# Block 0's rows: another order and eight DMA engines for the load, V written back in token order

## The chip, the cores and the metric

The kernel runs on one core of one Trainium2 chip. The metric is the device time of one execution in microseconds (us). Three runs of the kernel before gave 236.09, 236.26 and 236.44 us (median 236.26). The profiled execution took 236.12 us, of which 234.88 us lie between its first and its last instruction (its span); times inside the profile count from the span's start.

## The reference

One input x of 2048 tokens x 512 features (bf16) goes through a layer normalisation, and two branches are added to x:

```python
def _A_ref(x, wqkv, wo):        # 32 heads of 16, window of 8 tokens, every second token
    qkv = (x @ wqkv).reshape(B, S, 3, H, Dh) ...
    idx = pos[:, None] - (jnp.arange(8) * 2)[None, :]          # masked where < 0
    logits = einsum('bhsd,bhswd->bhsw', q, k[idx]) * scale     # softmax over w
    o = einsum('bhsw,bhswd->bhsd', attn, v[idx])
    return o.reshape(B, S, D) @ wo

def _B_ref(x, w_in, w_sp, b_sp, w_out):
    z = gelu(x @ w_in); z1, z2 = z[..., :896], layernorm(z[..., 896:])
    g = einsum('ts,bsf->btf', w_sp, z2) + b_sp[None, :, None]
    return (z1 * g) @ w_out

xn = layernorm(x)
return x + _A_ref(xn, A_wqkv, A_wo) + _B_ref(xn, B_w_in, B_w_sp, B_b_sp, B_w_out)
```

## The kernel before, in words

The 2048 tokens are 16 blocks of 128 rows; a block's rows lie on the 128 partitions. The kernel is written as a list of tasks, each with an engine, what it reads and writes, and an estimated time. A planner in the kernel's own code (`Plan.schedule`) puts the tasks of each engine into an order, by estimated times, priorities, a few landing times written in by hand and lists of names that must follow one another; `Plan.emit` then writes one instruction stream per engine with semaphore waits. SP, ACT and POOL issue the DMAs: plain loads and stores and DMA transposes on SP, block 0 and block 1 of x on ACT, V's write-back on POOL.

The start is what the change touches. TensorE first runs seven matmuls without use (`warm0` to `warm6`, L582), which keep it busy until x arrives. `ldx0` (L563, ACT's queue) loads block 0 of x, `ldx1` (L536, ACT's queue) block 1, `ldwv0` and `ldwv1` (L540, SP's queue) the two halves of V's weights, `ldx2`, `ldx3` and so on the rest (L536, SP's queue), `ldwin2a` and `ldwin2b` the weights of z2.

Blocks 0 to 2 take a short cut for V. TensorE transposes the raw rows by a matmul with an identity (`pe_tr`, L601; tasks `xTx0a`, `xTx0b`, `xTx0c` for block 0, `xTx1`, `xTx2`): the rows of x are the stationary operand, the identity is what is streamed. ACT copies the result out (L628, L632; the tile `xcT`), and V is computed from the raw transposed rows (L704; `V0_0`, `V0_0b`, `V0_1`). ACT evicts it with each row's factor 1/sigma (L712; `vraw`). Much later, when the sum over V's weight columns is known, VectorE takes away the mean's part for blocks 0 to 2 (`fix0` to `fix2`, L759), and the three blocks are written to `vscr` in DRAM (`Vw0` to `Vw2`, L691), one row of 512 elements per token. V of the other blocks goes there directly. Attention later reads `vscr` eight times shifted (`ldVs0` and on, L1005).

Meanwhile VectorE computes the mean and variance of each block's rows (`bnst0`, L621; `bnag0`, L623; `vpe0`, L636), POOL 1/sigma (L638), VectorE the normalised rows (`norm0`, L650; tile `xn`). Block 0's normalised rows are transposed on TensorE as well (`xTr0`, L601 again, between V1 and V2), and ACT copies them into `xnT` (L609); the other blocks go through DMA transposes (L644). From `xnT` come z2 (L836), Q and K (L728) and z1 (L882); then the spatial matmul (L982) and the output (L1038, L1047).

The order on TensorE at the start is written out by hand: warm0 to warm6, xTx0a, xTx0b, xTx0c, warm7, V0_0, V0_0b, xTx1, V0_1, xTx2, V1_0, V1_1, xTr0, V2_0, V2_1, z2_0 and so on.

Of the kernel before, what the change touches and what calls it, by code (L numbers as in the profile page):

```python
# [346 lines left out]
def build_kernel(nc, A_x, A_wqkv, A_wo, B_x, B_w_in, B_w_sp, B_b_sp, B_w_out, out, report=False, emit=True):  # L347
# [14 lines left out]
    x2 = A_x[0]  # L362
    o2 = out[0]

    vscr = nc.dram_tensor("vscr", (16 + S, 512), BF).ap()
# [45 lines left out]
    with ExitStack() as es:  # L411
# [5 lines left out]
        def A(name, n, o2_=0):  # L417
            return ar[:, off[name] + o2_: off[name] + o2_ + n]

        def AC(o_, dims):  # L420
            return bass.AP(tensor=ar, offset=o_, ap=[[AR, 128]] + [list(d) for d in dims])

        def Fv(name, n, o2_=0):
            return fp[:, foff[name] + o2_: foff[name] + o2_ + n]
# [7 lines left out]
        def P(bk, n, o_=0):  # L432
            return ps[:, bk.col(o_): bk.col(o_) + n]
# [65 lines left out]
        def c_mm(n):  # L499
            return max(26.0, n / 2.4 + 2.7)  # L500

        def c_act(n, psum=True, accum=False):
            return (170.0 if psum else 205.0) + n * 0.833 + (200.0 if accum else 0.0)
# [9 lines left out]
        def dma(eng, fn, nbytes, chan, reads=(), writes=(), name="", xbar=False, prio=0.0, after=()):  # L513
            return T(eng, fn, reads=reads, writes=writes, name=name, prio=prio, after=after,
                     dma=dict(chan=chan, nbytes=nbytes, xbar=xbar, iss=(1270.0 if nbytes < 400000 else 2200.0) if xbar else None))

        ident = A("ident", 128)
# [39 lines left out]
        def ld_wqk(which, eng):  # L557
# [2 lines left out]
                A_wqkv[:, 512 * which: 512 * which + 512].rearrange("(c p) n -> p c n", p=128)),  # L560
                512 * 512 * 2, ("wqk", which), writes=[("wqk", which)], name="ld%s" % ("qk"[which]))

        dma("act", lambda e: e.dma_start(A("xin", 512), x2[0:128, :]), 128 * 512 * 2, ("xin", 0),  # L563
            writes=[("xin0", 0), ("xin0", 1)], name="ldx0")
        ld_x(1, "act")
        ld_wv(0)
# [25 lines left out]
        cen = []  # L592
        vps = []

        def pe_tr(src, keys, name, dcs=(0, 1, 2, 3)):
            bk = plan.bank(name)

            def tr(t):
                last = None
                for dc in dcs:  # L600
                    last = t.matmul(P(bk, 128, 128 * dc), src[:, 128 * dc:128 * dc + 128], ident, start=True,  # L601
                                    stop=True)
                return last
            T("pe", tr, reads=keys + ["ident"], writes=[bk], est=len(dcs) * c_mm(128), name=name)
            return bk

        def to_xnT(b, bk, halves, prio=0, after=()):
            for d0, dn in (((0, 2), (2, 2)) if halves else ((0, 4),)):
                T("act", (lambda d0, dn: lambda a: a.activation(  # L609
                    AC(off["xnT"] + d0 * S + 128 * b, [[S, dn], [1, 128]]),  # L610
                    P(bk, 128 * dn, 128 * d0).rearrange("p (c n) -> p c n", c=dn), ACTF.Copy))(d0, dn),
                  reads=[bk], writes=([("xnT", b, d0 // 2)] if halves else [("xnT", b)]), est=c_act(128 * dn),
                  name="xTe%d_%d" % (b, d0), prio=prio)

        def ln_block(b):
            sl = b % 8
            xin = A("xin", 512, 512 * b)
            xn = A("xn", 512, 512 * sl)
            xk = [("xin", b)] if b else [("xin0", 0), ("xin0", 1)]

            T("dve", lambda v: v.bn_stats(Fv("st6", 6, 6 * b), xin), reads=xk, writes=[("st6", b)],  # L621
              est=685, name="bnst%d" % b, prio=b * 0.1)
            T("dve", lambda v: v.bn_aggr(Fv("mv", 2, 2 * b), Fv("st6", 6, 6 * b)), reads=[("st6", b)],  # L623
              writes=[("mv", b)], est=178, name="bnag%d" % b, prio=-1 + b * 0.1)
            if b < NRAW:
                bcs = [pe_tr(xin, xk, "xTx0a", (0,)), pe_tr(xin, xk, "xTx0b", (1,)), pe_tr(xin, xk, "xTx0c", (2, 3))] if b == 0 else [pe_tr(xin, xk, "xTx%d" % b)] * 2
                for c0 in (0, 1) if b == 0 else ():
                    T("act", (lambda c0, bc: lambda a: a.activation(A("xcT", 128, 128 * c0), P(bc, 128, 128 * c0), ACTF.Copy))(c0, bcs[c0]),  # L628
                      reads=[bcs[c0]], writes=[("xcTq", c0)], est=c_act(128), name="xTc0_0%s" % "ab"[c0], prio=-1)
                for h0, hn in ((1, 1),) if b == 0 else ((0, 1), (1, 1)) if b < 2 else ((0, 2),):  # L630
                    bc = bcs[-1 if b == 0 else h0]
                    T("act", (lambda h0, hn, bc: lambda a: a.activation(A("xcT", 256 * hn, 512 * b + 256 * h0),  # L632
                                                                        P(bc, 256 * hn, 256 * h0), ACTF.Copy))(h0, hn, bc),
                      reads=[bc], writes=[("xcT", b, hf) for hf in range(h0, h0 + hn)], est=c_act(256 * hn),
                      name="xTc%d_%d" % (b, h0), prio=-1)
            T("dve", lambda v: v.tensor_scalar(Fv("vpe", 1, b), Fv("mv", 1, 2 * b + 1), LN_EPS, None, ALU.add),  # L636
              reads=[("mv", b)], writes=[("vpe", b)], est=140, name="vpe%d" % b, prio=-1.5 + b * 0.1)
            lnr.append(T("pool", lambda g: g.tensor_tensor(Fv("rstd", 1, b), Fv("vpe", 1, b), Fv("mhalf", 1), ALU.pow),  # L638
                         reads=[("vpe", b), "mhalf"], writes=[("rstd", b)], est=550, name="rstd%d" % b, prio=0))
            norm(b)  # L640
            if b < NXT:
                to_xnT(b, pe_tr(xn, [("xn", sl)], "xTr%d" % b), b == 0)
                return None
            return dma("sp", lambda e: e.dma_start_transpose(AC(off["xnT"] + 128 * b, [[S, 4], [1, 128]]), xn),  # L644
                       128 * 512 * 2, ("xT", sl), reads=[("xn", sl)], writes=[("xnT", b)], name="xTd%d" % b,
                       xbar=True, prio=1)

        def norm(b, after=None):
            xin = A("xin", 512, 512 * b)
            norms.append(T("dve", lambda v: v.tensor_scalar(A("xn", 512, 512 * (b % 8)), xin, Fv("mv", 1, 2 * b),  # L650
                                                            Fv("rstd", 1, b), ALU.subtract, ALU.mult),
                           reads=([("xin", b)] if b else [("xin0", 0), ("xin0", 1)]) + [("mv", b), ("rstd", b)],
                           writes=[("xn", b % 8)], est=c_ts(512), name="norm%d" % b, prio=-1 + b * 0.1,
                           after=([after] if after is not None else ())))
# [33 lines left out]
        fixes = []  # L688

        def v_write(b, vn, vk):  # L690
            dma("pool", lambda e: e.dma_start(vscr[16 + 128 * b: 16 + 128 * b + 128, :], vn),  # L691
                128 * 512 * 2, ("vwr", b % 8), reads=[vk], writes=[("vscr", b)], name="Vw%d" % b, prio=1)

        def v_block(b):
# [61 lines left out]
        def fix_all():  # L756
            for b, vn, vk in fixes:
                def fix(b=b, vn=vn, vk=vk):
                    T("dve", lambda v: v.scalar_tensor_tensor(vn, ncs, Fv("mr", 1, b), vraw(b), ALU.mult, ALU.add),  # L759
                      reads=["ncs", "mr", ("vraw", b)], writes=[vk], est=690, name="fix%d" % b, prio=1)  # L760
                fix()
                v_write(b, vn, vk)
# [131 lines left out]
        for b in range(8, NB):  # L894
            lastx = ld_x(b)
        lnd = [ln_block(b) for b in range(NRAW)]
        mean_rstd()
        csbank = plan.bank("cs", 2)
        for b in range(NRAW):
            v_block(b)  # L900
        lnd += [ln_block(b) for b in range(NRAW, NB)]

        dma("pool", lambda e: e.dma_start(vscr[0:16, :], ar[0:16, off["zeros"]: off["zeros"] + 512]), 16 * 512 * 2,
# [39 lines left out]
        for j in range(NJ):  # L943
            for pr in PAIRS:
# [3 lines left out]
                                                             ap=[[0, 128], [1, S]])),  # L948
# [166 lines left out]
def bass_parallel_sum__sliding_local_dilated__mixer_gmlp__prompt_kernel(  # L1115
    nc, A_x, A_wqkv, A_wo, B_x, B_w_in, B_w_sp, B_b_sp, B_w_out, out
):
    build_kernel(nc, A_x, A_wqkv, A_wo, B_x, B_w_in, B_w_sp, B_b_sp, B_w_out, out)
# [28 lines left out]
```

## Time and profile before

| what | value |
|---|---|
| median of three runs | 236.26 us (236.09 to 236.44) |
| profiled execution | 236.12 us, span 234.88 us |
| TensorE (PE) busy | 230.9 us, 98% of the span |
| VectorE (DVE) busy | 207.2 us, 88% |
| ScalarE (ACT) busy | 96.0 us, 41% |
| L563, issue of block 0's load, on ACT | 0.80 us, 0.43 us long |
| from that issue to landing | 2.7 us |
| block 0's statistics (L621) start | 3.54 us |
| first transpose of block 0 (L601) starts | 3.65 us |
| first V matmul of block 0 (L704) starts | 4.37 us |
| L691, V's write-back: issue, landing | 0.54 us each, 4.0 us (median of 16) |

How to read it: PE is TensorE's matmuls, PEld its weight loads, which run beside them; a letter q behind an engine (ACTq, SPq) marks its instruction queue, where DMAs are issued. In the chain of work that ended last, each line is a start, a length and a group of instructions that followed one another; "issue" is time in which the engine waited for nothing that the profile shows. The ends of matmuls are modelled, their starts are recorded. A row of a transfer is one packet in the trace's packet records, and each DMA engine that took part reports its end by one update of the transfer's semaphore; the consumer waits for the last.

### The profile page before, as it was taken

The numbers are of one execution on the slowest core, as the hardware profiler recorded it, in microseconds if no ns is written. First come the engines' busy times: TensorE is split into PE (matmuls) and PEld (weight loads), VectorE is DVE, ScalarE is ACT, GpSimd is POOL, SyncE is SP. The second block draws the span as 40 slices with busy tenths as digits, with TensorE's granted clock in tenths as the row PEclk, the third lists the DMA queues.
The fourth block names the chain that finished last, engine by engine and source line by source line (L and its number), as shares of the span: only waits on it lengthen the run. The fifth ranks groups of instructions, "written<-read, shape, count | busy, mean of one in ns | idle before, by whom it ended". The sixth has DMA issues, their size and how long they took to land.

```text
span 234.9 us, 2982 instructions
## 1 busy us (share of the span) xinstructions
PE 230.9 (98%) x1107; PEld 109.0 (46%) x1127; DVE 207.2 (88%) x271; ACT 96.0 (41%) x144; POOL 29.3 (12%) x58
## 2 busy tenths in 40 slices
PE   8999999999999999999999999999999999999996
PEld 3545455544444444444444444444444444444443
DVE  4706899999999999999999999998899998999723
ACT  3798878888986589510020532011111111000000
POOL 2305640404261202000000000000000000000000
DMA  6769934999811275345299999999969959945442
GB/s 205 219 197 372 175 68 99 217 190 226 230 47 47 67 238 170 63 123 147 74 358 219 282 208 260 190 230 274 300 187 273 305 138 307 290 116 156 112 137 68
DMA packets 83991, 44.55 MB, mean 190 GB/s; under 512 B 56180, under 2 KB 83204, under 8 KB 83976
## 3 DMA queue, kind: packets, MB, share of 16 engines
q1 hardware_dynamic: 82744, 41.94, 70.6%
q0 software_dynamic: 800, 2.11, 2.9%
q10 hardware_dynamic: 432, 0.30, 0.4%
q8 instruction: 9, 0.15, 0.3%
q14 instruction: 6, 0.05, 0.1%
HBM read 26.62 MB, written 4.22 MB: 131 GB/s over the span
## 4 chain that ended last, share of the span: by engine, by line
PE 98%; issue 1%; DVE 0%; DVEq 0%
PE ps L982 41%; PE ps L728 12%; PE ps L836 10%; PE ps L882 10%; PE ps L1047 10%; PE ps L704 6%; PE ps L1038 6%; PE ps L582 1%; PE ps L772 1%; PE ps L601 1%; DVE arena L1053 0%; PE ps L783 0%; DVEq L325 0%
## 5 line engine op out<-in xcount | busy, mean ns | idle before, releaser
L982 PE MATMUL ps<-arena 128*128 128x512 bf16 x439 | 96.6, 379 | 0.5
L982 PEld LDWEIGHTS ps<-arena 128*128 128x128 bf16 x448 | 43.7, 98 | 53.1 <-issue 0.4
L990 ACT ACTIVATE arena<-ps 128x1024 bf16<-128x1024 f32 (+1 forms) x16 | 14.7, 917 | 76.9 <-PE ps L982 70.5
L749 DVE TENSOR_TENSOR arena<-arena 128x4096 bf16<-128x4096 bf16 x16 | 36.5, 2285 | 0.0
L1010 DVE TENSOR_TENSOR arena<-arena 128x4096 bf16<-128x4096 bf16 x16 | 36.5, 2286 | 0.0
L1013 DVE TENSOR_TENSOR arena<-arena 128x2048 bf16<-128x2048 bf16 (+1 forms) x32 | 30.1, 953 | 0.2
L728 PE MATMUL ps<-arena 128*128 128x512 bf16 x124 | 28.2, 379 | 0.3 <-issue 0.2
L754 DVE TENSOR_TENSOR arena<-arena 128x4096 bf16<-128x4096 bf16 x12 | 27.5, 2290 | 0.1
L1047 PE MATMUL ps<-arena 128*128 128x512 bf16 (+2 forms) x116 | 26.5, 366 | 0.1
L836 PE MATMUL ps<-arena 128*128 128x448 bf16 x128 | 25.5, 352 | 0.0
L882 PE MATMUL ps<-arena 128*128 128x512 bf16 x110 | 24.4, 379 | 0.1
L728 PEld LDWEIGHTS ps<-arena 128*128 128x128 bf16 x128 | 14.4, 113 | 13.3 <-ACT arena L718 0.4
L737 ACT ACTIVATE arena<-ps 128x1024 bf16<-128x1024 f32 x16 | 16.2, 1021 | 6.9 <-PE ps L728 6.8
L1053 DVE TENSOR_TENSOR arena<-ps,arena 128x512 bf16<-128x512 f32 (+2 forms) x17 | 11.2, 659 | 8.6 <-PE ps L1047 8.5
L836 PEld LDWEIGHTS ps<-arena 128*128 128x128 bf16 x128 | 12.5, 98 | 12.1
L1047 PEld LDWEIGHTS ps<-arena 128*128 128x128 bf16 x119 | 11.4, 98 | 12.8
L882 PEld LDWEIGHTS ps<-arena 128*128 128x128 bf16 x112 | 11.0, 98 | 13.2
L1038 PE MATMUL ps<-arena 128*128 128x512 bf16 (+2 forms) x68 | 16.6, 366 | 0.1
L704 PE MATMUL ps<-arena 128*128 128x512 bf16 x62 | 16.2, 391 | 0.1
L844 ACT ACTIVATE arena<-ps 128x896 bf16<-128x896 f32 x16 | 14.6, 913 | 3.4 <-PE ps L836 3.3
L621 DVE BATCH_NORM_STATS2 fpool<-arena 128x6 f32<-128x512 bf16 x16 | 10.7, 685 | 5.8 <-DMA arena<-in_A_x_dram 5.8
L888 ACT ACTIVATE arena<-ps 128x1024 bf16<-128x1024 f32 (+1 forms) x16 | 14.0, 919 | 4.4 <-PE ps L882 4.3
(65 smaller groups left out, 168.5 us busy)
## 6 DMA issues: line engine op xcount, KB each, us to landing
arena<-vscr SPq DMA_DIRECT2D x16, 1024.0 KB, 6.2
arena<-in_A_x_dram SPq DMA_DIRECT2D x30, 128.0 KB, 3.9
vscr<-arena POOLq DMA_DIRECT2D x16, 128.0 KB, 4.0
out_dram<-arena SPq DMA_DIRECT2D x15, 128.0 KB, 2.0
arena<-in_A_wqkv_dram SPq DMA_DIRECT2D x2, 512.0 KB, 4.5
arena<-in_B_w_in_dram SPq DMA_DIRECT2D x2, 448.0 KB, 5.1
arena<-in_B_w_in_dram SPq DMA_DIRECT2D x1, 896.0 KB, 8.3
arena<-in_B_w_out_dram SPq DMA_DIRECT2D x1, 896.0 KB, 5.6
```

Source lines behind the costliest of these rows:

```text
L704: last = t.matmul(P(bk, 512), A("xcT", 128, 512 * b + 128 * dc) if b < NRAW else xTv(b, dc), A("wv", 512, 512 * dc), start=(dc == 0), stop ...
L728: last = t.matmul(P(bk, 512, 512 * which), AC(off["wqk"] + 2048 * which + 512 * dc + c, [[4, 128]]), AC(off["xnT"] + dc * S + 512 * j, [[1 ...
L737: T("act", lambda a: a.activation(AC(qo, [[ko - qo, 2], [1, 512]]), P(bk, 1024).rearrange("p (t n) -> p t n", t=2), ACTF.Copy, scale=0.5), ...
L749: T("dve", (lambda pbv, qb, kb: lambda v: v.tensor_tensor(pbv, qb, kb, ALU.mult))(pbv, qb, kb), reads=rd, writes=[("pb", s_)], est=c_tt(40 ...
L754: T("dve", (lambda av, bv: lambda v: v.tensor_tensor(av, av, bv, ALU.add))(av, bv), reads=[("pb", 1)], writes=[("pb", acc)], est=c_tt(4096 ...
L836: last = t.matmul(P(bk, 448, 512 * hf), xTv(b, dc), AC(off["w_in2"] + 896 * dc + 448 * hf, [[1, 448]]), start=(dc == 0), stop=(dc == 3))
L882: last = t.matmul(P(bk, 512, 512 * i), AC(off["w_in1"] + 896 * dc + 128 * fc, [[1, 128]]), AC(off["xnT"] + dc * S + 512 * j, [[1, 512]]), ...
L982: last = t.matmul(P(bk, 512, 512 * i), AC(off["z2"] + FH * sh + 128 * fc, [[1, 128]]), AC(off["wT%d" % r_] + sh * 512, [[1, 512]]), start= ...
L1010: T("dve", lambda v: v.tensor_tensor(tv, tv, av, ALU.mult), reads=[("attn", b)], writes=[("Vs", sv)], est=c_tt(4096), name="pv%d" % b, pri ...
L1013: T("dve", (lambda n: lambda v: v.tensor_tensor(A("Vs", n, 4096 * sv), A("Vs", n, 4096 * sv), A("Vs", n, 4096 * sv + n), ALU.add))(n), wri ...
L1038: last = t.matmul(P(bk, cn), AC(off["OT"] + 512 * tb + 128 * cc, [[1, 128]]), AC(off["wo"] + 512 * cc + c0, [[1, cn]]), start=(cc == 0), s ...
L1047: last = t.matmul(P(bk, cn), AC(off["z1T"] + fc * S + 128 * tb, [[1, 128]]), AC(off["w_out"] + 512 * fc + c0, [[1, cn]]), start=False, sto ...
```

## The change

Three places change, all for block 0. The load `ldx0` reads the rows in another order: `rows0` turns the 128 rows into 8 groups of 16, the row 8q + a going to partition 16a + q. The leading dimension of the DMA's source is then 8 instead of 128, so the transfer is dealt to eight DMA engines instead of 16. Everything that works row by row (the statistics, the normalisation, the raw V of block 0, its correction) now works on the rows in the new order. Two steps bring the tokens back into order: `xTr0` streams the identity with its columns rearranged (column 8q + a of the result is row 16a + q), and `Vw0` writes the rows of V through the same `rows0` pattern.

```diff
-        dma("act", lambda e: e.dma_start(A("xin", 512), x2[0:128, :]), 128 * 512 * 2, ("xin", 0),
+
+        def rows0(ap):
+            return ap.rearrange("(q a) n -> a q n", a=8)
+
+        dma("act", lambda e: e.dma_start(A("xin", 512), rows0(x2[0:128, :])), 128 * 512 * 2, ("xin", 0),
             writes=[("xin0", 0), ("xin0", 1)], name="ldx0")
...
-        def pe_tr(src, keys, name, dcs=(0, 1, 2, 3)):
+        def pe_tr(src, keys, name, dcs=(0, 1, 2, 3), rhs=None):
             bk = plan.bank(name)
+            rhs = ident if rhs is None else rhs
...
-                    last = t.matmul(P(bk, 128, 128 * dc), src[:, 128 * dc:128 * dc + 128], ident, start=True,
+                    last = t.matmul(P(bk, 128, 128 * dc), src[:, 128 * dc:128 * dc + 128], rhs, start=True,
                                     stop=True)
...
-                to_xnT(b, pe_tr(xn, [("xn", sl)], "xTr%d" % b), b == 0)
+                to_xnT(b, pe_tr(xn, [("xn", sl)], "xTr%d" % b,
+                                  rhs=ident.rearrange("p (a q) -> p q a", a=8) if b == 0 else None), b == 0)
...
         def v_write(b, vn, vk):
-            dma("pool", lambda e: e.dma_start(vscr[16 + 128 * b: 16 + 128 * b + 128, :], vn),
+            rows = vscr[16 + 128 * b: 16 + 128 * b + 128, :]
+            dma("pool", lambda e: e.dma_start(rows0(rows) if b == 0 else rows, vn),
                 128 * 512 * 2, ("vwr", b % 8), reads=[vk], writes=[("vscr", b)], name="Vw%d" % b, prio=1)
```

The tasks, their engines, their estimates and the planner's inputs are the same, so every engine has the same instructions in the same order.

## The prediction

> **What bounds the kernel now.** I read the page first: span, shares, chain.
>
> ```profile
> span 234.9 us, 2982 instructions
> PE 230.9 (98%) x1107; PEld 109.0 (46%) x1127; DVE 207.2 (88%) x271; ACT 96.0 (41%) x144; POOL 29.3 (12%) x58
> ...
> PE 98%; issue 1%; DVE 0%; DVEq 0%
> ```
>
> TensorE is busy for 98% of the span and is 98% of the chain that ended last. So the change counts only through what it does to TensorE: how early its real work starts, how long its own instructions take, and whether it later waits. Next the chain in order of time over the first 9 us, where block 0 is worked on.
>
> ```profile
> 0.84 2.82 PE ps L582 x7
> 3.66 0.57 PE ps L601 x4
> 4.24 0.11 PE ps L582
> 4.34 0.03 issue
> 4.37 1.01 PE ps L704 x2
> 5.38 0.43 PE ps L601 x4
> 5.81 0.64 PE ps L704 x2
> 6.45 0.22 PE ps L601 x4
> 6.67 0.86 PE ps L704 x4
> 7.54 0.22 PE ps L601 x4
> ```
>
> L582 is warm-up work without use, L601 a transpose of four 128-column matmuls, L704 V. Two things are to be seen. First, the same four L601 matmuls take 0.43 us at 5.38 and 0.22 us at 6.45: TensorE runs at half speed until about 6.1 us. By the start times in the trace (5.605, 6.031, 6.288) the L704 matmul at 6.031 has a pitch of 0.257 us between the slow 0.427 and the fast 0.216; with t us of it slow, t + (0.427 - t) x 0.216/0.427 = 0.257 gives t = 0.08. Second, from 4.37 on the pieces join without a gap, and the start times go on so to 232.75: besides records that are missing, no matmul starts more than about 0.12 us late. A shift at the start therefore reaches the end.
>
> The third view is the timeline around block 0's arrival.
>
> ```profile
> 3.54 0.69 DVE L621 BATCH_NORM_STATS2 fpool<-arena 128x6 f32<-128x512 bf16 x1 [2.35 <-DMA arena<-in_A_x_dram]
> 3.62 0.35 PEld L601 LDWEIGHTS ps<-arena 128*128 128x128 bf16 x4 [0.55 <-issue]
> ...
> 3.95 0.45 ACT L628 ACTIVATE arena<-ps 128x128 bf16<-128x128 f32 x2 [0.71 <-PE ps L601]
> ...
> 4.34 0.21 PEld L704 LDWEIGHTS ps<-arena 128*128 128x128 bf16 x2 [0.27 <-issue]
> ```
>
> VectorE and TensorE both start block 0 right after its load (L563, issued at 0.80). Its sixteen semaphore updates in the trace come in two groups: eight at 2.78 to 2.86, eight at 3.36 to 3.52. The last one lets bnst0 go at 3.54 and the first weight load at 3.62. The warm-up would let TensorE go at 3.46 (its last matmul starts at 3.351, pitch 0.107). So the load holds TensorE for 0.19 us, no more; ACT's copy (3.95 to 4.23) then sets V0's start at 4.37.
>
> **The change part by part.**
>
> *The load.* Still 128 rows of 1 KB, but with a leading dimension of 8, so 16 rows on each of 8 engines instead of 8 on 16. An undisturbed row takes 46 ns in the packet records. The early group got its 8 rows done in 0.58 to 0.65 us (first packet 1.865, semaphore packets 2.443 to 2.523), because from 2.1 us wv's rows from SP's queue take turns with it. By 2.1 us five rows per engine are through; the other 11, taking turns, need 11 x 2 x 0.046 = 1.01, so 3.1 to 3.27 with the spread seen; 0.34 us from semaphore packet to landing gives 3.45 to 3.61, against 3.516. That holds if the eight are the early ones; I take it so, because a transfer that is dealt out from its first row on reaches the early group first, and eight engines counted from there are that group. The bounds: 0.74 us for 16 undisturbed rows lands at 2.95 (the gain stops at 0.19 us); a load that lies on few engines already, wo's (L964: four engines by its semaphore updates, 32 rows each), landed 3.0 to 3.7 us after issue, which here is 4.5. I take the middle of the first estimate, no shift.
>
> [...]
>
> *What a shift costs.* Start later by d while the clock rises at the same moment, and work worth d at half speed remains to be done at full speed: d/2. If the clock's rise moves along, it is d.
>
> *What follows on the queues.* Early engines get 8 rows more, 0.37 us, late ones as much less. Their landings say what that meets: wv's second half landed at 4.44 to 4.92 and 4.98 to 5.30, and would land at 4.8 to 5.3 and 4.6 to 4.9; V0_1 needs it at 5.6. x1 (4.38, needed at 5.18 by TensorE, 4.55 by VectorE) and x2 (5.64, needed at 6.29) keep theirs within 0.1. Cost nothing, while that cover of 0.2 us or more holds. wo's loads, on fewer engines too, were issued in 0.53 to 0.62 us against 0.43: 0.1 to 0.2 us more on ACT's queue in front of x1's issue, the table load and the first activation; these end at 3.24, ACT is first needed at 3.95, cover 0.7.
>
> *The identity read.* xTr0 (7.54 above) must undo the order: its four matmuls now stream the identity with a step of 16 elements, 32 bytes. TensorE has no gap there, so every ns counts, four times. No matmul of the trace streams with such a step; the nearest is the weight load that reads with a step of 4 elements:
>
> ```profile
> L728 PEld LDWEIGHTS ps<-arena x128: 112/113/132, 17.6 to 78.5; 128*128 128x128 bf16 x128
> L836 PEld LDWEIGHTS ps<-arena x128: 97/98/98, 8.2 to 64.2; 128*128 128x128 bf16 x128
> ```
>
> 15% more: 4 x 55 x 0.15 = 0.03 us. At half rate, the pace of the slow clock above, it is 0.43 - 0.22 = 0.21 us. I take 0.2, since the step is four times as wide; zero and 0.66 (quarter rate: 4 x 3 x 0.055) are the ends.
>
> [...]
>
> *V's write-back.* Vw0 goes out on POOL at 89.17 with the same 128 rows, in token order; it landed at 91.18, and its reader ldVs0 is issued on SP at 103.02. Even at three times its 2 us, cover remains: nothing. Statistics, raw V and the correction of block 0 are per row and move with the rows.
>
> *Sum, of the profiled run* (236.12 us, span 234.88): + 0 (load) + 0.2 (identity) = 236.3. The median of the three is 236.26, so 236.45. 0.2% is 0.47 us, about what a measurement can tell.
>
> **Rivals.**
>
> *Early data, early clock.* Block 0 lands by 3.35 and fills the 0.19 us hole. For it: half of its rows are there at 2.86. On its own that is worth 0.1 to 0.19. To be seen, the clock must rise earlier: TensorE stood idle at 3.46 and again at 4.14 to 4.37, and if unbroken work is what raises it, one hole less may bring it forward. From 4.37 to 6.11 it works 1.74 us at half speed; all of that at full speed saves 0.87. Against: the second hole stays, and V0 still needs ACT's copy. Half of it, 0.44, and 0.19, leave out any cost of the identity: 235.6.
>
> [...]
>
> *The eight are the slow ones* (the slower side). Place: block 0's landing. If the second group is the eight, 8 rows more cost 0.37 us alone or 0.74 taking turns: landing 3.9 to 4.25, V0 at 4.75 to 5.1. By half or whole that is 0.19 to 0.74 at the end, plus 0.2 for the identity: 236.65 to 237.2, say 236.9. It decides once the landing is past about 3.85 with the clock moving along. For it: the second group stood still from 2.4 to 2.8, when the DMA share fell:
>
> ```profile
> 1.80:2.40 0.60, 0.60 (x3) 0.15 (x1) 0.00 (x0) 0.60 (x1) 0.00 (x0) 1.00 0.72 217
> 2.40:2.80 0.40, 0.40 (x2) 0.15 (x1) 0.00 (x0) 0.40 (x1) 0.00 (x0) 1.00 0.62 200
> 2.80:3.50 0.70, 0.70 (x3) 0.15 (x1) 0.00 (x0) 0.43 (x2) 0.00 (x0) 1.00 1.06 356
> ```
>
> (the last two columns are DMA share and GB/s), and if descriptors are what was missing, sixteen rows in a row for one engine after the other can be late on any eight.
>
> [...]
>
> *A clock that rises later.* A wider hole before 4.37 leaves TensorE too idle, and the rise comes late by 2 us or more: half of that, 1 us and up, 237.5.
>
> *It does nothing:* rows still spread over 16, and the step is free: 236.26.
>
> **How the numbers follow.** Forecast 0.38 (236.1 to 236.8; 0.05 of it slower by over 0.2%), nothing 0.07, early 0.24 (0.22 faster by over 0.2%), slow eight 0.24 (0.22 slower by over 0.2%), late clock 0.07. Faster 0.22, same 0.33 + 0.07 + 0.02 + 0.02 = 0.44, slower 0.05 + 0.22 + 0.07 = 0.34. The range leaves out the late clock and the outer end of the early case: 235.5 to 237.1. The forecast is 236.45.
>
> **What would show it.** In the profile after: bnst0's start (3.54: same; 3.3: early; 3.9 or more: slow eight); x0's time to landing (2.7); the four L601 matmuls of xTr0 (0.22: free; 0.43: half rate); the place where four L601 matmuls go from 0.43 to 0.22 (the clock); joined pieces after that. I am wrong if TensorE waits anywhere after 8 us, or if the clock's rise moves by over 0.5 us.

## The result, and the profile after

The changed kernel is slower. Six runs of it, beside six of the kernel before, gave 237.37, 237.76, 238.97, 239.17, 239.20 and 239.32 us (median 239.07) against a median of 236.15 (235.82 to 236.44): a ratio of 1.0105, with an interval of 1.0072 to 1.0139. The forecast was 236.45, in a range up to 237.1. The profiled execution is the shortest of the six, 237.37 us, with a span of 236.1; what makes the others longer comes with the experiments.

The page of the changed kernel, span, shares and chain:

```profile
span 236.1 us, 2982 instructions
PE 230.8 (98%) x1107; PEld 108.5 (46%) x1127; DVE 207.4 (88%) x271; ACT 96.0 (41%) x144; POOL 29.4 (12%) x58
...
PE 96%; DMA 2%; issue 1%; ACTq 0%; DVE 0%; DVEq 0%
```

TensorE is busy for as long as before, but the chain is now 96% TensorE and 2% a DMA. The chain of waits over the first microseconds says which (lines have moved: L567 is the issue of block 0's load, L586 the warm-up, L606 the transposes, L711 V, L843 z2; L626 is the statistics):

```profile
0.80 1.18 ACTq L567
1.98 0.04 issue
2.02 4.08 DMA arena<-in_A_x_dram
6.10 0.05 issue
6.15 0.40 PE ps L606 x4
6.55 0.43 PE ps L711 x2
6.98 0.22 PE ps L606 x4
7.20 0.86 PE ps L711 x4
8.07 0.92 PE ps L606 x4
8.99 0.86 PE ps L711 x4
9.86 1.32 PE ps L843 x7
```

Before, this stretch began with the warm-up matmuls. Now it begins with ACT's issue of block 0's load, which takes 1.18 us; behind it the load of block 1 (x1) goes out at 2.02, lands at 6.10, and TensorE waits for that. The four L606 matmuls at 8.07 are `xTr0` with the stepped identity: 0.92 us, where they took 0.22. The timeline around block 0:

```profile
0.80 1.18 ACTq L567 DMA_DIRECT2D arena<-in_A_x_dram  x1
2.02 0.35 ACTq L536 DMA_DIRECT2D arena<-in_A_x_dram  x1
4.79 0.69 DVE L626 BATCH_NORM_STATS2 fpool<-arena 128x6 f32<-128x512 bf16 x1 [3.60 <-DMA arena<-in_A_x_dram]
4.81 0.23 PEld L606 LDWEIGHTS ps<-arena 128*128 128x128 bf16 x4 [1.73 <-DMA arena<-in_A_x_dram]
5.41 0.61 PE L711 MATMUL ps<-arena 128*128 128x512 bf16 x2
```

Block 0's statistics start at 4.79 (before 3.54) and V at 5.41 (4.37). The load's semaphore gets eight updates by engines, at 4.13 to 4.76, in place of sixteen at 2.78 to 3.52; a ninth, at 2.07, comes as the issue ends and before the first row, which is at 2.91 in the packet records (1.87 before). TensorE stands idle from 3.46 to 4.81.

The sum of this one execution closes. From V's first matmul to z2's first, TensorE has twelve V matmuls of 0.216 us and twelve transposing ones of 0.056: 3.26 us at the fast clock. Before, 0.83 us came on top, for the stretch at half speed up to 6.11: 4.37 + 3.26 + 0.83 = 8.46, where z2's first matmul starts. After, all of it ran at the fast clock (0.056 us from one transposing matmul to the next from 4.81 on), with 0.30 us of waiting for x1 and 0.70 for the identity: 5.41 + 3.26 + 0.30 + 0.70 = 9.67, and the trace has 9.69. What comes after z2's first matmul is the same 227.7 us in both executions (236.12 - 8.46 and 237.37 - 9.69). So everything is decided before z2.

### The profile page after: what moved, and what is told of

It reads as the page before. It is cut to its first block, busy times and chain, and to the rows that moved or that the text cites. A ratio compares the mean times of both kernels' runs of the same rounds, so it can differ in the third digit from the quotient of the medians.

```text
span 236.1 us, 2982 instructions
## 1 busy us (share of the span) xinstructions
PE 230.8 (98%) x1107; PEld 108.5 (46%) x1127; DVE 207.4 (88%) x271; ACT 96.0 (41%) x144; POOL 29.4 (12%) x58
## 4 chain that ended last, share of the span: by engine, by line
PE 96%; DMA 2%; issue 1%; ACTq 0%; DVE 0%; DVEq 0%
PE ps L989 41%; PE ps L735 12%; PE ps L843 10%; PE ps L889 10%; PE ps L1054 10%; PE ps L1045 6%; PE ps L711 6%; DMA arena<-in_A_x_dram 2%; PE ps L779 1%; PE ps L606 1%; ACTq L567 0%; DVE arena L1060 0%; PE ps L790 0%; DVEq L325 0%
## 5 line engine op out<-in xcount | busy, mean ns | idle before, releaser
L843 PE MATMUL ps<-arena 128*128 128x448 bf16 x128 | 25.5, 352 | 0.0
L843 PEld LDWEIGHTS ps<-arena 128*128 128x128 bf16 x128 | 12.5, 98 | 12.1
L626 DVE BATCH_NORM_STATS2 fpool<-arena 128x6 f32<-128x512 bf16 x16 | 10.7, 686 | 7.3 <-DMA arena<-in_A_x_dram 7.3
L711 PE MATMUL ps<-arena 128*128 128x512 bf16 x62 | 15.5, 379 | 0.2
```

What stands on the lines that cost most here:

```text
L711: last = t.matmul(P(bk, 512), A("xcT", 128, 512 * b + 128 * dc) if b < NRAW else xTv(b, dc), A("wv", 512, 512 * dc), start=(dc == 0), stop ...
L843: last = t.matmul(P(bk, 448, 512 * hf), xTv(b, dc), AC(off["w_in2"] + 896 * dc + 448 * hf, [[1, 448]]), start=(dc == 0), stop=(dc == 3))
```

## The experiments

The theory: the load's pattern is slow in itself (a long issue, a late landing, x1 behind it), the identity's step costs 0.7 us, the write-back nothing, and the moment at which the clock rises makes the spread from run to run. The rivals: the eight engines are the cause; the far-apart rows are; the competition with SP's loads is; or x1's last engine, and not the clock, makes the long runs. In each experiment `rows0` and `ident` are those of the diff; line numbers move by a few lines from kernel to kernel.

### One part of the change at a time

**The identity alone** (kernel before, only `xTr0` with the stepped identity, so that block 0's tokens stand in another order in `xnT`):

```diff
+  rhs=ident.rearrange("p (a q) -> p q a", a=8) if b == 0 else None   # xTr0
```

> The kernel before with one edit: xTr0 streams the rearranged identity (step of 16 elements), the load and V's write-back as before, so the tokens of block 0 stand in another order in xnT. Theory (the identity read runs at a quarter of the rate, and TensorE has no gap to hide it): the four L606 matmuls of xTr0 take 0.92 us instead of 0.22, the span grows by 0.7 us, 236.85 against 236.15, and all runs lie close together. Rival (xTr0's slow pace in the profile after comes from the late data or the clock around it): 0.22 us, 236.15.

Eleven runs: median 236.48 (236.13 to 237.06), ratio 1.0025 (1.0016 to 1.0034), which is 0.4 to 0.8 us; 0.7 was expected, the medians are 0.52 apart. In the trace the four matmuls start at 7.442, 7.654, 7.886 and 8.117, and V's next at 8.349: 0.91 us for 0.22.

**The load alone** (block 0's tokens stay in the new order):

```diff
-  dma("act", lambda e: e.dma_start(A("xin", 512), x2[0:128, :]), ...
+  dma("act", lambda e: e.dma_start(A("xin", 512), rows0(x2[0:128, :])), ...
```

> The kernel before with one edit: only the load of block 0 in the new order on eight engines; identity and V's write-back plain, so block 0's tokens stay in the new order. Theory (the load is what delays the start, and its idle hole leaves the clock to chance): issue 1.18 us, landing at about 4.8, x1 at about 6.1, no slow xTr0; runs of two kinds, 236.7 and 238.4, that is the times of the kernel after less 0.7. Rival (the long runs come from the write-back or the identity): one kind, 236.6 to 236.9.

Five runs: 238.07 (237.71 to 238.72), ratio 1.0095 (1.0079 to 1.0111). Issue 1.20 us, block 0 landed at 4.81, x1 at 6.45. It is most of the change, and more than the later start of V (5.66 against 4.37) explains: this execution ran at half speed until 7.98. The runs do not fall into the two kinds that were expected.

**The write-back alone** (V's rows of block 0 lie in another order in `vscr`):

```diff
-  e.dma_start(vscr[16 + 128 * b: 16 + 128 * b + 128, :], vn)
+  e.dma_start(rows0(rows) if b == 0 else rows, vn)               # Vw0
```

> The kernel before with one edit: only Vw0 writes its rows through the rearranged pattern, so V's rows of block 0 lie in another order. Theory (write-back hidden): landing about 1.8 us later than before, at about 93, reader issued at 103, time unchanged within 0.1 us. Rival (POOL's longer descriptor work or eight engines in a busy stretch delay something): 0.3 us or more slower.

Eleven runs: 236.10 (235.66 to 236.46), ratio 1.0005 (0.9996 to 1.0013). Free. It landed at 91.81, 0.6 us later than before and not the 1.8 that was expected.

Against the kernel before beside them, the medians of the three parts are 0.52, 2.11 and 0.14 us longer, 2.77 together; the whole change is 2.92 longer.

### What a step in the streamed operand costs

The kernel before, with the four matmuls of `xTr0` streaming the identity with steps of 2, 4, 8 and 32 elements (block 0's tokens then stand in four other orders):

```diff
+  rhs=[ident.rearrange("p (a q) -> p q a", a=a_) for a_ in (64, 32, 16, 4)]
```

> The kernel before, but the four matmuls of xTr0 stream the identity with steps of 2, 4, 8 and 32 elements (4, 8, 16 and 64 bytes), so block 0's tokens stand in other orders in the four parts of xnT. Theory (reads that leave a 16-byte line each time pay, all the same): pitch 0.056 at steps 2 and 4, 0.23 at 8 and 32 as at 16. Rival (cost grows with the step): 0.06, 0.07, 0.12, 0.4 or so.

One run, 235.83 us. From start to start, one matmul each: 0.058 us for a step of 2 elements (4 bytes), 0.095 for 4, 0.229 for 8, 0.221 for 32; without a step it is 0.056, and with 16 elements, in the kernel after, 0.232. So in these runs the price climbs up to a step of 16 bytes (0.229 us) and beyond it stays at about four times the 0.056.

**The changed kernel without that price:** VectorE copies the rearranged identity once into a tile of its own, `identP`, and `xTr0` streams that:

```diff
+  T("dve", lambda v: v.tensor_copy(identP.rearrange("p (q a) -> p q a", a=8),
+                                   ident.rearrange("p (a q) -> p q a", a=8)), ...)
-  rhs=ident.rearrange("p (a q) -> p q a", a=8) if b == 0 else None
+  rhs=identP if b == 0 else None
```

> The kernel after, but VectorE first copies the rearranged identity into a tile of its own, before x arrives, and xTr0 streams that copy without a step; the computation is whole. Theory (step): xTr0 back to 0.22 us, both kinds of runs 0.7 us shorter than the kernel after: 236.7 and 238.4. Rival (the quarter rate is not the step's): no change against the kernel after, 237.4 and 239.1.

Six runs: 238.67 (237.68 to 238.76), ratio 1.0103 (1.0087 to 1.0119). In the trace `xTr0` is back at its old pace:

```profile
9.35 0.22 PE ps L609 x4
```

The median shows less of it. It is 2.71 us above the kernel before beside it, where the changed kernel is 2.92 above, and 2.84 in a later group of runs: 0.1 to 0.2 us won, not 0.7, from groups of five and six runs that overlap. The step's price is shown on TensorE, but how much of it a typical run pays stays open between this and the 0.52 us of the identity alone. The load's part stays whole: block 0 at 4.83, x1 at 6.41, and half speed until 8.51.

### Why the load is late: engines, distance of rows, or pattern

**Sixteen engines with such a pattern** (the kernel with `identP`, 16 groups of 8 rows):

```diff
-  return ap.rearrange("(q a) n -> a q n", a=8)
+  return ap.rearrange("(q a) n -> a q n", a=16)     # and identP likewise
```

> The kernel with the copied identity (e4), but 16 groups of 8 rows instead of 8 groups of 16: the load still in another order, on 16 engines, the computation whole. Theory (eight engines are what slows the issue and the start of the transfer): issue back to about 0.43 us, landing at about 3.5, 236.1. Rival (the three-dimensional order is what costs): issue 1.2 us, landing at 4.5 or later, 237.7 to 238.8 as in e4.

Six runs: 237.25 (236.52 to 238.33), ratio 1.0058 (1.0036 to 1.0081).

```profile
0.80 0.63 ACTq L570 DMA_DIRECT2D arena<-in_A_x_dram  x1
1.47 0.59 ACTq L539 DMA_DIRECT2D arena<-in_A_x_dram  x1
5.40 0.70 DVE L629 BATCH_NORM_STATS2 fpool<-arena 128x6 f32<-128x512 bf16 x1 [3.57 <-DMA arena<-in_A_x_dram]
```

The issue falls to 0.63 us, but block 0 lands at 5.38, later than with eight engines; its sixteen updates are spread from 3.59 to 5.38. So the number of engines alone is not the cause. It does count in the time: these runs are 1.35 us above the kernel before, those on eight engines 2.71.

**Neighbouring rows, in the same form of pattern** (the kernel before; block 0 holds other rows of x):

```diff
+  ap=[[17 * 512, 8], [512, 16], [1, 512]]     # near8: 8 groups of 16 neighbours, 17 rows apart
+  ap=[[9 * 512, 16], [512, 8], [1, 512]]      # near16: 16 groups of 8 neighbours, 9 rows apart
```

> The kernel before, but block 0 is loaded as 8 groups of 16 neighbouring rows, the groups 17 rows apart (so every 17th row is left out and block 0 holds partly other tokens); identity and write-back plain. The pattern has three dimensions and a leading 8, as in the kernel after, but each group reads 16 KB in a row. Theory A (the form of the pattern, its leading 8, is what is slow): issue 1.2 us on ACT, landing near 4.8, time as e2, 237.7 to 238.7. Theory B (the far-apart rows are slow to fetch): issue 1.2 or less, landing by 3.9, 236.0 to 237.

> As e9_near8, but 16 groups of 8 neighbouring rows, 9 rows apart: three dimensions, 16 engines. Theory A (any pattern that cannot be walked in two dimensions costs, eight engines cost more): issue 0.63 us and landing 4.5 to 5.4 as in e5. Theory B (rows far apart): landing at 3.5, 236.0.

```profile
0.80 1.18 ACTq L563 DMA_DIRECT2D arena<-in_A_x_dram  x1
...
4.65 0.69 DVE L621 BATCH_NORM_STATS2 fpool<-arena 128x6 f32<-128x512 bf16 x1 [3.45 <-DMA arena<-in_A_x_dram]
```

```profile
0.80 0.63 ACTq L563 DMA_DIRECT2D arena<-in_A_x_dram  x1
...
4.67 0.69 DVE L621 BATCH_NORM_STATS2 fpool<-arena 128x6 f32<-128x512 bf16 x1 [3.48 <-DMA arena<-in_A_x_dram]
```

The first view is near8, the second near16. near8: 238.42 (237.30 to 239.20), ratio 1.0101 (1.0064 to 1.0137), issue 1.18, block 0 at 4.63, x1 at 6.14: as in the changed kernel. near16: 237.78 (236.53 to 238.59), ratio 1.0064 (1.004 to 1.0088), issue 0.63, block 0 at 4.65, x1 at 5.58. So on ACT, with SP's loads beside it, the pattern of two levels over rows landed late in every profile, at 4.63 to 5.38 against 3.52, whichever rows it named. With sixteen engines the one profile of far-apart rows is later than the one of neighbouring rows (5.38 against 4.65); with eight there is hardly a difference (4.63 against 4.64 to 4.95 in five profiles of the changed kernel). The length of the issue does not set the landing: behind an issue of 0.63 us the first row comes at 2.81 and 2.89, behind one of 1.18 to 1.20 at 2.69 to 2.91. Why it is so late behind the shorter one stays open.

**The load on SP's queue** (kernel with `identP`, `ldx0` first on SP, ahead of V's weights):

```diff
-  dma("act", lambda e: e.dma_start(A("xin", 512), rows0(x2[0:128, :])), ...
+  dma("sp", lambda e: e.dma_start(A("xin", 512), rows0(x2[0:128, :])), ...
```

> e4 with the load of block 0 as the first on SP's queue instead of ACT's; SP's other loads come one place later, ACT's queue begins with block 1. Theory A (the pattern's issue is slow on any queue): about 1.2 us on SP, landing about 4.7, wv 0.7 later, time as e4 or slower. Theory B (ACT's issue waited for SP's, which was using the descriptor hardware at the same time): 0.5 to 0.6 us as wo's loads on SP, landing about 3.3 to 3.6, 236.0 to 236.6.

Four runs: 238.40 (238.15 to 238.57), ratio 1.0104 (1.009 to 1.0119).

```profile
0.80 0.80 SPq L570 DMA_DIRECT2D arena<-in_A_x_dram  x1
0.81 0.37 ACTq L539 DMA_DIRECT2D arena<-in_A_x_dram  x1
...
9.93 0.93 PE L846 MATMUL ps<-arena 128*128 128x448 bf16 x4 [1.49 <-DMA arena<-in_B_w_in_dram]
```

Block 0 lands at 3.66 and x1, now first on ACT, at 2.88. But every load on SP goes out about 0.8 us later, the first half of z2's weights lands at 9.88 instead of 7.51, and TensorE waits at z2. The wait has moved.

**SP's loads held back** (kernel with `identP`; V's weights and what follows wait for the tile of the identity, until 1.55 us):

```diff
+  reads=["ident"]     # ldwv0, ldwv1; then ldx2, ldx3, ldwin2a, ... in that order
```

> e4 with SP's loads held until POOL has made the identity (about 1.55 us), so that ACT issues block 0's load with nothing else being issued. Theory A (the pattern itself is slow to issue on ACT): 1.0 us or more. Theory B (it waited for SP's issues): 0.45 to 0.8 us as on SP's queue in e8, first data near 1.9.

One run, 236.97 us.

```profile
0.81 1.20 ACTq L570 DMA_DIRECT2D arena<-in_A_x_dram  x1
1.55 0.96 SPq L543 DMA_DIRECT2D arena<-in_A_wqkv_dram  x2
...
3.68 0.69 DVE L629 BATCH_NORM_STATS2 fpool<-arena 128x6 f32<-128x512 bf16 x1 [1.84 <-DMA arena<-in_A_x_dram]
```

The issue stays at 1.20, so that is not a wait for SP; but the first row comes at 2.30 and block 0 lands at 3.65, 1.2 us earlier than in the kernel with `identP` as it was. So the late landing is the pattern and SP's loads together: the pattern makes the load slow to get its first row out (2.30 against 1.87 in the kernel before), and when SP's loads come in ahead of it, it loses another 1.2 us. z2 starts at 8.43, as before, but TensorE now waits 0.2 us each for x1 and for V's second half of weights and 0.8 us within z2, for its weights and for block 1's transposed rows.

### The clock, and the spread from run to run

**The hole filled** (kernel with `identP`, nine long warm-up matmuls instead of six, up to 4.7 us):

```diff
-  NWARM = 7
+  NWARM = 10       # n_ = 512 if wi < 9 else 128
```

> e4 with nine long warm-up matmuls instead of six, so that TensorE is busy until about 4.8 us, when block 0 lands; computation whole. Theory (the long runs of after and e4 are runs in which the idle hole from 3.46 to 4.81 keeps the clock down for another stretch): block 0 as late as in e4, but all runs short and close together, about 237.0, and no slow L609 matmuls after 6.2 us. Rival (the long runs come from transfers that land late by chance): two kinds as in e4, 237.7 to 238.8.

Five runs: 237.44 (237.31 to 237.67), ratio 1.0064 (1.0052 to 1.0076). No real matmul runs at half speed, and the runs lie within 0.36 us of each other. What is left is x1 (landed at 6.36; TensorE waits 0.39) and, at 10.9, a wait of 0.3 us for block 1's transposed rows in z2, which come from x1 as well.

**A hole made** (kernel before, three long warm-up matmuls instead of six):

```diff
-  NWARM = 7
+  NWARM = 4        # n_ = 512 if wi < 3 else 128
```

> The kernel before with three long warm-up matmuls instead of six: TensorE idle from about 2.2 us until block 0 lands at 3.5; nothing else changes. Theory (clock): the real work starts when it did, but the clock rises later, between about 5.8 and 9.2 us by run, so 0.5 to 2 us slower, 236.5 to 238.1, spread wide. Rival (warm-up time is without effect, only arrival counts): 236.0, spread as before.

Six runs: 236.30, 237.46, 237.59, 237.67, 237.67 and 237.78 us; median 237.63, ratio 1.0062 (1.0045 to 1.008).

```profile
0.80 2.72 DMA arena<-in_A_x_dram
3.52 0.05 issue
3.56 0.61 PE ps L601 x4
...
4.31 1.01 PE ps L704 x2
5.32 0.43 PE ps L601 x4
...
8.73 0.43 PE ps L601 x4
```

The data come as before and V starts at 4.31, even 0.06 earlier. But the four L601 matmuls take 0.43 us even at 8.73; the half speed lasts until about 9.6. Taking away work that computes nothing costs 1.7 us in the median.

**The changed kernel again, and with the hole filled:**

> The kernel after once more, unchanged, to see how its runs are spread and to get a second profile of it. Theory (the clock's moment is a matter of chance, and the idle hole lets it slip by one stretch in most runs): runs of two kinds again, about 237.4 to 237.8 and 239.0 to 239.3, and a profile of a long run shows half-speed matmuls after 6.2 us, to 8 us or later. Rival (the long runs are the transfers'): long runs with an early clock and with transfers that land 1.5 us later than in the first profile.

> The kernel after with nine long warm-up matmuls instead of six, which fill the hole until block 0 lands at 4.8; nothing else. Theory: only short runs, 237.3 to 237.9, close together. Rival: two kinds as in the kernel after.

The changed kernel, five more runs: 238.96 (238.02 to 239.42), ratio 1.0129 (1.0114 to 1.0144). With nine long warm-up matmuls, beside it on the same chip: 237.53, 237.57, 237.59, 237.63, 238.29 and 238.38 us, median 237.61, ratio 1.0067 (1.0055 to 1.0079). The hole's late clock is worth 1.35 us in the median. The two longer runs are another matter; the profile is of the run of 238.38:

```profile
2.06 5.05 DMA arena<-in_A_x_dram
7.10 0.05 issue
7.15 0.40 PE ps L606 x4
7.54 0.43 PE ps L711 x2
```

From V on the clock is fast, but x1 landed at 7.10 instead of 6.10, and TensorE waited 1.18 us.

**Three more runs of the changed kernel,** for the profile of one of its long runs:

> The changed kernel again, one look, to profile one of its longer runs. If the clock's moment decides a run's length: a run near 239 us shows pitches of 0.107 us between V's first matmuls until 8 us or later, and a run near 237.5 us has them at 0.056 from the first real matmul on. If x1's last engine decides instead: a run near 239 us shows TensorE waiting over 1.5 us for x1 with a fast clock throughout.

> As for the look before: a long run with a late clock, or a long run with a late x1; the length should follow from 0.5 us for each us at half speed after 4.8 us, plus TensorE's wait for x1.

> As for the two looks before it, for a third draw of the clock's moment and of x1's landing.

They were of 239.17, 238.33 and 238.32 us. With the two before them, and the kernel before (times in us; "half speed" is where real matmuls are 0.107 or 0.427 us apart instead of 0.056 or 0.216):

| profiled run | V starts | wait for x1 | half speed | z2 starts | run less z2's start |
|---|---|---|---|---|---|
| before, 236.12 | 4.37 | none | to 6.11 | 8.46 | 227.66 |
| after, 237.37 | 5.41 | 0.30 | none | 9.69 | 227.68 |
| after, 238.02 | 5.35 | 0.84 | none | 10.17 | 227.85 |
| after, 238.32 | 5.35 | 0.15 | to 8.02 | 10.67 | 227.65 |
| after, 238.33 | 5.49 | 0.11 | to 7.93 | 10.67 | 227.66 |
| after, 239.17 | 5.60 | 0.53 | 6.91 to 9.68 | 11.49 | 227.68 |

Both theories of the long runs hold a part. The last column is constant but for one run, so a run's length is set by z2's start, and each of those is, to 0.05 us, V's start + 3.26 + the wait + 0.70 + half of the time that TensorE works at half speed. For 239.17: 5.60 + 3.26 + 0.53 + 0.70 + 1.39 = 11.48, against 11.49. From one run of the changed kernel to another the clock makes up to 1.4 us and x1 up to 0.7.

The run of 239.17 shows the clock rise early and fall again. The windows of its trace (stretch, its length, TensorE busy and matmuls, granted clock, DMA share, GB/s):

```profile
3.50:6.91 3.41, 1.54 (x14) 1.00 1.09 303
6.91:9.68 2.77, 2.77 (x12) 0.50 0.67 233
9.68:10.32 0.64, 0.64 (x4) 0.50 0.15 37
```

From 3.50 to 6.91 the clock is full, but block 0 and x1 keep TensorE idle for more than half of it; for the next 3.41 us the clock is at 0.50. A trap in this view: in the run of 238.33, matmuls are at half speed until 7.93 while the column shows 1.00 throughout, since that trace has no record of the clock. The distances between starts decide.

What took the full clock away in the run of 239.17 is not shown: the idle stretches in 3.50 to 6.91 are 1.5, 0.3 and 0.5 us, and half speed then lasts from 6.91 to 10.32.

## Why the prediction was wrong, step by step

**What held.** The change acts only through TensorE's start and its own instructions: the time after z2's first matmul is unchanged to 0.02 us in four of five profiles. The write-back is free (in the profiled execution it landed at 92.99 instead of 91.18, and its reader is issued 11 us later). What follows on SP's queue keeps its cover: V's weights landed at 3.69 and 5.26. The view that the place to watch is block 0's landing, with an expected sign of bnst0 at "3.9 or more", was right; it is 4.79.

**The load term failed ("no shift", 3.45 to 3.61).** It counted rows per engine from a first row at 1.87, as in the kernel before, so the time up to the first row was put at no change. That step failed: the issue went from 0.43 to 1.18 us, the first row from 1.87 to 2.91, and the landing from 3.52 to 4.76, outside its upper end of 4.5. A longer issue is not the whole of it, since the first row is as late behind an issue of 0.63 us. The step "0.1 to 0.2 us more on ACT's queue" was the row that pointed there, wo's loads, and it was used only for what is queued behind; it measured 0.75. With it fell the step on x1 ("keep theirs within 0.1"): x1 lands 1.7 us later and is waited for, 0.11 to 0.84 us.

**The identity term was too small.** The mechanism was right, the size 0.2 instead of 0.70, beyond even the outer end of 0.66. The half rate was taken for want of a row, when the only row near it was 15% on a step of 8 bytes; for the streamed operand the runs show 0.095 us at 8 bytes and 0.229 at 16. The steps measured above are that missing row. In the medians the term is less certain than in the trace: 0.52 us from the identity alone, 0.1 to 0.2 from taking the step away.

**The clock was a rival at 0.07 and is in three of five profiles.** "A clock that rises later" was written down with its mechanism, but as an alternative to a late block 0, and its "2 us or more" had no row behind it (half speed ended at 7.93 and 8.02 in two profiles, instead of 6.11); in truth a late block 0 is what makes the hole. The two should have been one case, with its price added: the profiles of after have V 0.98 to 1.23 us later, a wait for x1 of 0.39 on average and 0.70 for the identity, some 2.2 us in all, of 2.92 between the medians. That would leave 0.8 to the clock. The other way round, filling the hole brings back 1.35 us, and the kernel before loses 0.83 to half speed in its own profile, which makes 0.5. The two do not quite meet, since both take a typical run from few profiles. How often each moment of the clock comes up was not measured.

**"The eight are the slow ones" was right in its sign and wrong in its reason.** Landing at 3.9 to 4.25 was too early (4.76), and sixteen engines with a pattern of the same form (ratios 1.0058 and 1.0064) are late too. Beside the kernel before, with its one plain dimension of 128, the two are 1.35 and 1.62 us longer in the median.

None of the variants with the rows in another order beats the kernel before; the nearest, with SP's loads held back, took 236.97 us in its one run.

## What to carry to other kernels

Another row order of a DMA was not free in its issue (1.18 us against 0.43): before a load is turned into a pattern of two levels, look at how long such an issue takes on its queue and at what is queued behind it, above all for the first load of a kernel. When late data would leave TensorE idle during its warm-up, add the late clock to the late data instead of weighing one against the other, and cover the hole with work that computes nothing; here that brought back 1.35 us in the median. Rearrange an operand once into a tile of its own rather than stream it with a step of 16 bytes or more where TensorE has no gap: the step cost 0.7 us in the trace, though the copy won back only 0.1 to 0.2 in the median.

## What the runs showed of the hardware that was not expected

- The issue of the same 128 rows of 1 KB took 0.43 us on ACT as one dimension of 128, 0.63 as 16 x 8 and 1.18 to 1.20 as 8 x 16; the last took 0.80 on SP.
- A matmul that streamed with a step of 32 bytes took 0.232 us at the full clock and 0.230 to 0.237 at half (the four at 9.68 in the run of 239.17): in these runs its pace did not go with TensorE's clock, so at half speed, where one without a step took 0.107, the step cost 0.5 us instead of 0.7.
- The moment of the clock differs from profile to profile, and no run shows what it goes by. In the run of 239.17, TensorE was busy for 1.54 of the 3.41 us from 3.50 on (0.45), and the clock stood at 0.50 for the 3.41 us that followed. With a hole made, TensorE was busy for 6.41 of the 6.60 us from 3.4 to 10, and half speed still lasted until about 9.6. The busy times are as the profile counts them, with modelled ends of matmuls; no run was made to find a threshold.
